# Deep cross network, last layer: one row tile from its own x, another's sums laid into its bank

## The chip, the cores and the metric

The kernel runs on one core of a Trainium2 chip. The metric is device time in microseconds (us) of one launch. Times of the kernel before: 128.68 us median of 3 runs (128.41 to 128.70).

## The reference

Six cross layers on a batch of 4096 rows with 416 features, all in bfloat16:

```python
B, F, D, L = 4096, 26, 16, 6
Din = min(F * D, 1024)          # 416
def reference(x0, ws, bs):      # (4096, 416), (6, 416, 416), (6, 416)
    x = x0
    for l in range(ws.shape[0]):
        x = x0 * (x @ ws[l] + bs[l]) + x
    return x
```

Written out, the state after layer l is x0 times (1 + the sum over the layers so far of x_i W_i + b_i). The kernel before uses this form throughout: it adds the products of all layers up in PSUM and never clears them between layers.

## The kernel before, in words

**Blocks and layout.** The batch is cut into four blocks of 1024 rows (`s` = 0 to 3), each in two halves of 512 rows (`h`). In a block the state is kept transposed: features on partitions, rows along the free dimension. 416 features are three chunks of 128 (`c`) and a tail of 32; the four quarters of a block's tails share 128 partitions. One block after the other passes through all six layers (`l`). Block 3 passes through five of them in this layout; its last layer is written by hand behind the loop.

**A layer.** `main` (L319) multiplies a chunk of W by the state into the bank of half h and chunk m, `bank(h, m)`, banks 0 to 5; `tail_rows` (L335) adds the tail's part to all banks; `tail_outs` (L377) computes the tail's own outputs in banks 6 and 7. `leave` (L428, instruction at L435) on VectorE reads a bank, adds the sum of biases so far (plus one), multiplies by x0 and writes the next state `xT_sb`. `leave_tail` (L450) does the same for the tail: two ScalarE reads (L445) and a GpSimd product (L458).

**The last layer of block 3.** It gives rows on partitions, so that the result can be stored as it is. Block 3's sums of layers 0 to 4, which stand transposed in banks 0 to 5, are first copied with the bias to `sS_sb` by `keep_sum` (L464, instructions at L467 and L469), and the tail's to `st_sb` on GpSimd (L584). For each of eight row tiles of 128 rows (`j`), `row_main` (L617) computes x W into one bank, `row_sums` (L627) adds the tile's old sums to it by multiplying `sS_sb` by an identity matrix, which turns them, and `row_tails` (L639) adds the tail's part to all eight tiles. `finish` (L661) multiplies by x0's rows (`xr_sb`) and writes `o_sb`: on VectorE for six of the tiles (L665), and through a ScalarE copy (L672) and a GpSimd product (L676) for tiles 1 and 3. `store_rows` (L680) sends the rows out on the sync queue or ScalarE's.

**Order.** Every operation is put in a list of its engine by `Plan.add`, in the order in which the program calls it; each engine runs its list in that order. Waits come from the keys that an operation reads and writes. Readers of one PSUM bank also wait for each other. A DMA waits on the engine that issues it. In the last layer the written order on TensorE is: `row_main` of tiles 0 to 3 (in 32-column pieces), `row_sums` of the same, `row_tails`, then `row_main` and `row_sums` of each of the tiles 4 to 7, whole.

**The sync queue.** Blocks 0 to 2 leave through DMA transposes: three of 128x1024 (L475), one of 128x256 for the tails (L480), later a store of 832 KB (L492). The next blocks come in by transposes from DRAM (L205, L211).

Instruction lines in the profile are those of the lines inside the functions; all matmuls of the layers have line L287.

Of the kernel before, what the change touches and what calls it, by code (L numbers as in the profile page):

```python
# [6 lines left out]
FP32 = mybir.dt.float32  # L7
ALU = mybir.AluOpType
ACTF = mybir.ActivationFunctionType
# [109 lines left out]
def bass_standalone__dcn_v2_cross__recsys_kernel(  # L119
# [6 lines left out]
    B, D = x0.shape  # L126
    L = ws.shape[0]
    NC = 3
    DF = 128 * NC
# [3 lines left out]
    NS = B // SB  # L133
    H = SB // 2
# [5 lines left out]
    CH = range(NC)  # L140

    with ExitStack() as es:

        def sb(name, shape, dt=BF16):
            return es.enter_context(nc.sbuf_tensor(name, shape, dt))
# [7 lines left out]
        xr_sb = sb("xr_sb", [128, JS, D])  # L153
        x0T_sb = sb("x0T_sb", [128, NC, B])
        x0t_sb = sb("x0t_sb", [128, NS, 2, G])
        xT_sb = sb("xT_sb", [128, 2, NC, SB])
        xt_sb = sb("xt_sb", [128, 2, 2, G])
        t32_sb = sb("t32_sb", [128, 2, G], FP32)
        sS_sb = sb("sS_sb", [128, NC, SB])
        st_sb = sb("st_sb", [128, G])  # L160
        f32_sb = sb("f32_sb", [128, 2, D], FP32)
        xo_sb = sb("xo_sb", [128, NS - 1, NC, SB])
        xot_sb = sb("xot_sb", [128, NS - 1, G])
        ot_sb = sb("ot_sb", [128, NS - 1, 2, 128])
# [19 lines left out]
        def bank(h, m):  # L184
            return NC * h + m


        def load(queue, dst, src, name, writes):
            P.add(queue, lambda e: e.dma_start(dst, src), writes=writes, dma=name)
# [76 lines left out]
            ), reads=[("ones",)], writes=[("u",)],  # L266
        )
        P.add("gpsimd", lambda e: e.memset(wc_sb[:, :, :], 0.0), writes=[("wc", "wt%d" % i) for i in range(3)])

        def replicate():  # L270
            for g, eng in ((1, "gpsimd"), (3, "scalar"), (2, "gpsimd")):
# [156 lines left out]
        def leave(s, l, h, c):  # L428
            if l == L - 1:
                dst, key = xo_sb[:, s, c, h * H:(h + 1) * H], ("xo", s, c, h)  # L430
            else:
                dst, key = xT_sb[:, (l + 1) % 2, c, h * H:(h + 1) * H], ("xT", (l + 1) % 2, c, h)
            o = s * SB + h * H
            P.add(
                "vector", lambda e: e.scalar_tensor_tensor(  # L435
                    out=dst, in0=ps[:, bank(h, c), :], scalar=cb_sb[:, c, l:l + 1], in1=x0T_sb[:, c, o:o + H],
                    op0=ALU.add, op1=ALU.mult,
                ), reads=[("ps", bank(h, c)), ("cb",), ("x0T", s, c, h)], writes=[key],
            )
# [22 lines left out]
                swap(xt_sb[:, (l + 1) % 2], key, ("scalar", "gpsimd", "scalar", "gpsimd"))  # L462

        def keep_sum(h, c, eng):  # L464
            o, i, b = sS_sb[:, c, h * H:(h + 1) * H], ps[:, bank(h, c), :], cb_sb[:, c, L - 1:L]
            if eng == "scalar":
                fn = lambda e: e.activation(out=o, in_=i, func=ACTF.Identity, bias=b)  # L467
            else:
                fn = lambda e: e.tensor_scalar_add(o, i, b)  # L469
            P.add(eng, fn, reads=[("ps", bank(h, c)), ("cb",)], writes=[("sS", c, h)])  # L470

        def transpose_block(s):
            for c in CH:
# [10 lines left out]
        def store_block(s):  # L484
            P.add(
                "gpsimd", lambda e: e.tensor_copy(
                    out=o_sb[:, s * JS:(s + 1) * JS, DF:D].rearrange("p (g r) f -> p r g f", r=2),
                    in_=ot_sb[:, s, :, :].rearrange("p r (g f) -> p r g f", f=DR),
                ), reads=[("ot", s)], writes=[("oc", s)],
            )  # L490
            P.add(
                "sync", lambda e: e.dma_start(out_v[:, s * JS:(s + 1) * JS, :], o_sb[:, s * JS:(s + 1) * JS, :]),  # L492
                reads=[("o", s), ("oc", s)], writes=[("out", s)], dma="out%d" % s,
            )
# [48 lines left out]
        for s in range(NS):  # L543
            for l in range(L):
                ending = s == NS - 1 and l == L - 2
                if s == NS - 1 and l == L - 1:
                    break
                if s == 0 and l == 0:
                    for k in CH:
                        for part in range(2) if k == 0 else (None,):  # L550
                            for m in CH:
                                main(s, l, 0, m, k, part)
                        if k == 1:
                            tail_in()
                            bias_sums()
                    tail_rows(s, l, True)
                    for c in CH:
                        leave(s, l, 0, c)
                    tail_outs(s, l, False)
                else:  # L560
                    for m in CH:
                        for k in CH:
                            main(s, l, 0, m, k)
                    tail_rows(s, l, l == 0)
                    for c in CH:
                        leave(s, l, 0, c)
                    tail_outs(s, l, False)
                if s == 0 and l == 1:
                    corner(2, L, "wt2")
                leave_tail(s, l, not ending)  # L570
                if l == 2 and 0 < s < NS - 1:
                    place_tail(s + 1)
                if s == 0 and l == 0:
                    corner(1, 2, "wt1")
                if l == 3 and s > 0:
                    store_block(s - 1)
                if ending:
                    P.add(
                        "gpsimd", lambda e: e.tensor_tensor(
                            out=bt_sb[:, :], in0=cb_sb[:, NC, L - 1:L], in1=cb_sb[:, NC, L - 2:L - 1], op=ALU.subtract  # L580
                        ), reads=[("cb",)], writes=[("bt",)],
                    )
                    P.add(
                        "gpsimd", lambda e, t=t32_sb[:, l % 2, :]: e.tensor_scalar_add(st_sb[:, :], t, bt_sb[:, :]),  # L584
                        reads=[("t32", l % 2), ("bt",)], writes=[("st",)],
                    )
                    for c in CH:
                        keep_sum(0, c, "scalar")
                for m in CH:
                    for k in CH:  # L590
                        main(s, l, 1, m, k)
                    leave(s, l, 1, m)
                if ending:
                    for c in CH:
                        keep_sum(1, c, ("scalar", "scalar", "vector")[c])
            if s < NS - 1:
                transpose_block(s)
            if s < NS - 2:
                load_transposed(s + 2, 0, SB)
                load_last_columns(s + 2)  # L600
            if s == NS - 2:
                load("sync", xr_sb[:, :, :], x0_v[:, (NS - 1) * JS:NJ, :], "xr", [("xr",)])


        s, l = NS - 1, L - 1
        ROW_BANKS = (6, 7, 0, 1, 2, 3, 4, 5)
        src, off = src_main(s, l)
        srct, tkey = src_tail(s, l)

# [17 lines left out]
        def row_sums(j, narrow):  # L627
            b, h = ROW_BANKS[j], j // 4

            def fn(pe):  # L630
                for c in CH:
                    ins = row_mm(
                        pe, ps[:, b, c * 128:(c + 1) * 128], sS_sb[:, c, j * 128:(j + 1) * 128], ident[:, :], False, narrow
                    )
                return ins

            P.add("tensor", fn, reads=[("ident",)] + [("sS", c, h) for c in CH], adds=[("ps", b)])
# [23 lines left out]
        def finish(j, by_pool):  # L661
            b, jj = ROW_BANKS[j], (NS - 1) * JS + j
            if by_pool is None:
                P.add(
                    "vector", lambda e: e.tensor_tensor(  # L665
                        out=o_sb[:, jj, :], in0=ps[:, b, 0:D], in1=xr_sb[:, j, :], op=ALU.mult
                    ), reads=[("ps", b), ("xr",)], writes=[("ol", j)],
                )
                return
            t = f32_sb[:, by_pool, :]  # L670
            P.add(
                "scalar", lambda e: e.activation(out=t, in_=ps[:, b, 0:D], func=ACTF.Copy),  # L672
                reads=[("ps", b)], writes=[("f32", by_pool)],
            )
            P.add(
                "gpsimd", lambda e: e.tensor_tensor(out=o_sb[:, jj, :], in0=t, in1=xr_sb[:, j, :], op=ALU.mult),  # L676
                reads=[("f32", by_pool), ("xr",)], writes=[("ol", j)],
            )

        def store_rows(queue, a, b):  # L680
            ja = (NS - 1) * JS
# [2 lines left out]
                reads=[("ol", j) for j in range(a, b)], writes=[("outl", a)], dma="outl%d" % a,  # L684
            )

        for j in range(4):
            row_main(j, True, True)
        for j in range(4):
            row_sums(j, True)  # L690
        row_tails()
        finish(0, None)
        finish(1, 0)
        finish(2, None)
        finish(3, 1)
        for j in range(4, 8):
            row_main(j, False, False)
            row_sums(j, False)
            finish(j, None)
        STORES = (("scalar", 2, 3), ("sync", 0, 2), ("sync", 4, 6), ("sync", 3, 4), ("scalar", 6, 7), ("sync", 7, 8))  # L700
        for queue, a, b in STORES:
            store_rows(queue, a, b)
        P.add("sync", None, reads=[("out", s) for s in range(NS - 1)] + [("outl", a) for _, a, _ in STORES])
# [30 lines left out]
```

## Time and profile before

| | |
|---|---|
| median of 3 runs | 128.68 us |
| the profiled execution | 128.06 us |
| its span, first to last instruction | 126.6 us |
| TensorE busy | 123.0 us, 97% of the span |
| VectorE busy | 99.6 us, 79% |
| ScalarE busy | 43.6 us, 34% |
| GpSimd busy | 38.8 us, 31% |
| TensorE clock granted | 1.00 |
| chain that ended last, TensorE's share | 97% |

PE is TensorE's matmuls, PEld its weight loads, DVE VectorE, ACT ScalarE, POOL GpSimd, SPq and ACTq the DMA queues of the sync engine and of ScalarE. Times in views are us from the span's start; a mean duration is in ns. A line of a timeline gives the start, the time from the first start to the last end of the instructions merged into it, and their number. The profiled execution's time is its span and 1.46 us around it.

### The profile page before, as it was taken

The page shows a single profiled execution, that of the slowest core. Times are in us where ns is not written, and L with a number is a line of the kernel's source. Part 1 is how long each engine was busy: PE and PEld are TensorE (multiplying, and loading weights), DVE is VectorE, ACT ScalarE, POOL GpSimd, SP SyncE. Part 2 cuts the span into 40 slices and gives each one's busy share as a digit, 9 for nine tenths or more (in the row PEclk, how much of TensorE's full clock was granted, in tenths as well). Part 3 has the DMA queues.
Part 4 walks back from the last instruction along what each step waited for, and adds up shares of the span by engine and source line. Part 5 has one row for each costly group of instructions (what it writes and reads, how often), then busy time and mean ns, then how long its engine had stood idle before and what let it go on. Part 6 is the DMA issues. An engine that isn't in the chain of part 4 may idle for free.

```text
span 126.6 us, 5307 instructions
## 1 busy us (share of the span) xinstructions
PE 123.0 (97%) x2414; PEld 64.3 (51%) x2414; DVE 99.6 (79%) x156; ACT 43.6 (34%) x95; POOL 38.8 (31%) x81
## 2 busy tenths in 40 slices
PE   7999999999999999999999999999999999999991
PEld 5554554554555554545545545545545545555660
DVE  2467978879879779779779789788797797797873
ACT  2342523424205225225205224233223252253820
POOL 6505404314204124144014043152122241350450
PEclk9999999999999999999999999999999999999999
DMA  3998998100059791016037893108009480006117
GB/s 99 237 240 226 292 199 107 28 19 0 8 114 161 167 166 28 22 54 226 0 86 169 68 218 87 31 5 269 5 9 203 80 257 0 5 0 226 49 39 236
DMA packets 34934, 14.03 MB, mean 111 GB/s; under 512 B 25722, under 2 KB 34912, under 8 KB 34912
## 3 DMA queue, kind: packets, MB, share of 16 engines
q1 hardware_dynamic: 33744, 13.20, 47.3%
q10 hardware_dynamic: 1136, 0.49, 1.4%
q8 instruction: 19, 0.31, 1.0%
q14 instruction: 3, 0.02, 0.1%
q0 software_dynamic: 32, 0.01, 0.0%
HBM read 3.79 MB, written 3.41 MB: 57 GB/s over the span
## 4 chain that ended last, share of the span: by engine, by line
PE 97%; DVE 0%; issue 0%
PE ps L287 94%; PE ps L295 2%; PE ps L506 1%; DVE o_sb L665 0%
## 5 line engine op out<-in xcount | busy, mean ns | idle before, releaser
L435 DVE SCALAR_TENSOR_TENSOR xT_sb<-ps,cb_sb,x0T_sb 128x512 bf16<-128x512 f32 x120 | 80.9, 743 | 16.5 <-PE ps L287 16.5
L287 PE MATMUL ps<-xT_sb,w_sb 128*32 128x512 bf16 (+1 forms) x1596 | 84.2, 364 | 0.0
L287 PEld LDWEIGHTS ps<-xT_sb,w_sb 128*32 128x32 bf16 x1596 | 40.9, 97 | 37.2 <-issue 4.0
L445 ACT ACTIVATE t_sb<-ps,cb_sb 64x256 f32<-64x256 f32 x46 | 21.6, 469 | 57.2 <-PE ps L287 56.9
L458 POOL TENSOR_TENSOR xt_sb<-t_sb,x0t_sb 128x256 bf16<-128x256 f32 x20 | 13.4, 671 | 65.2 <-ACT t_sb L445 65.2
L422 ACT ACTIVATE xt_sb<-xt_sb 32x256 bf16<-32x256 bf16 x38 | 15.7, 414 | 15.1 <-POOL xt_sb L458 14.9
L287 PE MATMUL ps<-x0T_sb,w_sb 128*32 128x512 bf16 (+1 forms) x348 | 18.6, 358 | 0.1
L424 POOL COPY xt_sb<-xt_sb 32x256 bf16<-32x256 bf16 x38 | 14.9, 392 | 2.4
L435 DVE SCALAR_TENSOR_TENSOR xo_sb<-ps,cb_sb,x0T_sb 128x512 bf16<-128x512 f32 x18 | 12.1, 743 | 2.5 <-PE ps L287 2.5
L287 PEld LDWEIGHTS ps<-x0T_sb,w_sb 128*32 128x32 bf16 x348 | 8.8, 96 | 7.5 <-issue 0.8
L287 PE MATMUL ps<-xt_sb,wt_sb 32*128 32x512 bf16 (+1 forms) x152 | 11.6, 326 | 0.0
L287 PE MATMUL ps<-xt_sb,wc_sb 32*128 32x256 bf16 x76 | 7.3, 268 | 0.0
L287 PEld LDWEIGHTS ps<-xt_sb,wt_sb 32*128 32x128 bf16 x152 | 2.3, 91 | 8.1 <-DVE xT_sb L435 8.1
L458 POOL TENSOR_TENSOR xot_sb<-t_sb,x0t_sb 128x256 bf16<-128x256 f32 x3 | 2.0, 671 | 9.9 <-ACT t_sb L445 9.9
L287 PE MATMUL ps<-w_sb,xT_sb 128*32 128x416 bf16 (+1 forms) x60 | 5.1, 339 | 0.0
L665 DVE TENSOR_TENSOR o_sb<-ps,xr_sb 128x416 bf16<-128x416 f32 x6 | 3.4, 587 | 1.3 <-PE ps L287 1.0
L287 PEld LDWEIGHTS ps<-xt_sb,wc_sb 32*128 32x128 bf16 x76 | 3.9, 93 | 0.2
L295 PE MATMUL ps<-const-bfloat16-1.0 128*128 128x256 bf16 x14 | 3.1, 414 | 0.8 <-PEq L719 0.8
L516 DVE COPY x0T_sb<-ps 128x256 bf16<-128x256 bf16 x6 | 1.3, 282 | 2.4 <-PE ps L506 2.4
L467 ACT ACTIVATE sS_sb<-ps,cb_sb 128x512 bf16<-128x512 f32 x5 | 3.0, 691 | 0.0
L287 PEld LDWEIGHTS ps<-w_sb,xT_sb 128*32 128x32 bf16 (+1 forms) x60 | 2.3, 97 | 1.4 <-issue 0.2
L676 POOL TENSOR_TENSOR o_sb<-f_sb,xr_sb 128x416 bf16<-128x416 f32 x2 | 1.9, 978 | 2.9 <-ACT f_sb L672 2.9
(43 smaller groups left out, 28.2 us busy)
## 6 DMA issues: line engine op xcount, KB each, us to landing
out_dram<-o_sb SPq DMA_DIRECT2D x3, 832.0 KB, 4.4
w_sb<-in_ws_dram SPq DMA_DIRECT2D x5, 312.0 KB, 3.9
xr_sb<-in_x_dram SPq DMA_DIRECT2D x1, 832.0 KB, 5.1
wt_sb<-in_ws_dram SPq DMA_DIRECT2D x4, 104.0 KB, 3.2
out_dram<-o_sb SPq DMA_DIRECT2D x2, 208.0 KB, 2.2
w_sb<-in_ws_dram SPq DMA_DIRECT2D x3, 104.0 KB, 3.7
xin_sb<-in_x_dram ACTq DMA_DIRECT2D x1, 208.0 KB, 3.4
xin_sb<-in_x_dram SPq DMA_DIRECT2D x1, 208.0 KB, 3.1
```

The source lines that it names most:

```text
L287: return pe.matmul(dst, lhsT=lhsT, rhs=rhs, start=start, stop=True, skip_group_check=True, tile_position=pos,)
L295: ins = pe.matmul(ps[:, 7, 0:256], lhsT=const[:, 0:128], rhs=const, start=True, stop=True)
L422: fn = lambda e, d=dst, s=src: e.activation(out=d, in_=s, func=ACTF.Copy)
L424: fn = lambda e, d=dst, s=src: e.tensor_copy(out=d, in_=s)
L435: "vector", lambda e: e.scalar_tensor_tensor(out=dst, in0=ps[:, bank(h, c), :], scalar=cb_sb[:, c, l:l + 1], in1=x0T_sb[:, c, o:o + H], op ...
L445: "scalar", lambda e, p=p, h=h: e.activation(out=dst[p, :], in_=ps[p, T_BANK[h], 0:G], func=ACTF.Identity, bias=cb_sb[p, NC, l:l + 1]), re ...
L458: "gpsimd", lambda e: e.tensor_tensor(out=dst, in0=t, in1=x0t_sb[:, s, 0, :], op=ALU.mult),
L467: fn = lambda e: e.activation(out=o, in_=i, func=ACTF.Identity, bias=b)
L506: ins = pe.transpose(out=psT[:, b, j * 128:(j + 1) * 128], in_=xin_sb[:, 2 * i + j, c * 128:(c + 1) * 128], identity=ident[:, :],)
L516: "vector", lambda e, d=dst, s=src: e.tensor_copy(out=d, in_=s),
L665: "vector", lambda e: e.tensor_tensor(out=o_sb[:, jj, :], in0=ps[:, b, 0:D], in1=xr_sb[:, j, :], op=ALU.mult), reads=[("ps", b), ("xr",)], ...
L676: "gpsimd", lambda e: e.tensor_tensor(out=o_sb[:, jj, :], in0=t, in1=xr_sb[:, j, :], op=ALU.mult),
```

## The change

In the last layer of block 3, two of the eight row tiles no longer get their old sums from TensorE.

Tile 0 is computed in the reference's own form, x0 (x W + b) + x. Its x is fetched by three DMA transposes of the state (128 rows of each chunk) into `xl_sb`. GpSimd forms z = x0 b in layer 3 of block 3, from a broadcast load of the last bias row, then y = z + x. Tile 0 is finished by ScalarE and GpSimd: product with x0, then the sum with y. The tail columns of y are zero, since the tail's sums are still added by `row_tails`.

Tile 3 (`LAID`) gets its sums by three DMA transposes out of `sS_sb` into `sr_sb`; ScalarE copies them into tile 3's bank, and `row_main` of tile 3 adds to what lies there. It is put behind `row_sums` of tiles 1 and 2.

To this end the sums of half 0 are kept earlier, chunk 2 first, between VectorE's `leave` operations and ahead of the tail's reads on ScalarE, and without the first 128 rows; banks of the row tiles, the engines that finish tiles 0 and 1, and the stores are reordered; the store of block 2 is issued a layer earlier.

```diff
+        P.add("gpsimd", lambda e: e.memset(y_sb[:, 1, DF:D], 0.0), writes=[("yz",)])
+        P.add("gpsimd", lambda e: e.memset(sr_sb[:, DF:D], 0.0), writes=[("srz",)])
...
         def keep_sum(h, c, eng):
-            o, i, b = sS_sb[:, c, h * H:(h + 1) * H], ps[:, bank(h, c), :], cb_sb[:, c, L - 1:L]
+            lo = 0 if h else 128
+            o, i, b = sS_sb[:, c, h * H + lo:(h + 1) * H], ps[:, bank(h, c), lo:H], cb_sb[:, c, L - 1:L]
...
+        def transpose_sums(col):
+            for c in (2, 0, 1):
+                P.add(
+                    "sync", lambda e, c=c: e.dma_start_transpose(
+                        sr_sb[:, c * 128:(c + 1) * 128], sS_sb[:, c, col:col + 128]
+                    ), reads=[("sS", c, 0)], writes=[("sr",)], dma="sr",
+                )
+
+        def transpose_first():
+            for c in CH:
+                P.add(
+                    "sync", lambda e, c=c: e.dma_start_transpose(
+                        xl_sb[:, c * 128:(c + 1) * 128], xT_sb[:, (L - 1) % 2, c, 0:128]
+                    ), reads=[("xT", (L - 1) % 2, c, 0)], writes=[("xl",)], dma="xl",
+                )
...
                     tail_rows(s, l, l == 0)
-                    for c in CH:
-                        leave(s, l, 0, c)
+                    if ending:
+                        leave(s, l, 0, 0)
+                        keep_sum(0, 2, "scalar")
+                        keep_sum(0, 0, "scalar")
+                        leave(s, l, 0, 1)
+                        leave(s, l, 0, 2)
+                        keep_sum(0, 1, "scalar")
+                        transpose_sums(H - 128)
+                        transpose_first()
+                    else:
+                        for c in CH:
+                            leave(s, l, 0, c)
                     tail_outs(s, l, False)
...
-                if l == 3 and s > 0:
+                if s > 0 and l == (3 if s < NS - 1 else 2):
                     store_block(s - 1)
+                if s == NS - 1 and l == 3:
+                    P.add(
+                        "gpsimd", lambda e: e.tensor_tensor(
+                            out=y_sb[:, 0, 0:DF], in0=xr_sb[:, 0, 0:DF], in1=bl_sb[:, :], op=ALU.mult
+                        ), reads=[("xr",), ("bl",)], writes=[("z",)],
+                    )
                 if ending:
...
-                    for c in CH:
-                        keep_sum(0, c, "scalar")
+                    P.add(
+                        "gpsimd", lambda e: e.tensor_tensor(
+                            out=y_sb[:, 1, 0:DF], in0=y_sb[:, 0, 0:DF], in1=xl_sb[:, :], op=ALU.add
+                        ), reads=[("z",), ("xl",)], writes=[("y",)],
+                    )
...
+                load("sync", bl_sb[:, :], bs[L - 1:L, 0:DF].to_broadcast([128, DF]), "bl", [("bl",)])
...
-        ROW_BANKS = (6, 7, 0, 1, 2, 3, 4, 5)
+        ROW_BANKS = (0, 1, 6, 2, 7, 3, 4, 5)
+        LAID = 3
...
+            t, o = f32_sb[:, by_pool, :], o_sb[:, jj, :]
+            mid = o if j else p_sb[:, :]
...
+                "gpsimd", lambda e: e.tensor_tensor(out=mid, in0=t, in1=xr_sb[:, j, :], op=ALU.mult),
+                reads=[("f32", by_pool), ("xr",)], writes=[("ol", j) if j else ("p",)],
+            )
+            if not j:
+                P.add(
+                    "gpsimd", lambda e: e.tensor_tensor(out=o, in0=mid, in1=y_sb[:, 1, :], op=ALU.add),
+                    reads=[("p",), ("y",), ("yz",)], writes=[("ol", j)],
+                )
...
-        for j in range(4):
+        for j in range(LAID):
             row_main(j, True, True)
-        for j in range(4):
+        for j in range(1, LAID):
             row_sums(j, True)
+        P.add(
+            "scalar", lambda e: e.activation(out=ps[:, ROW_BANKS[LAID], 0:D], in_=sr_sb[:, :], func=ACTF.Copy),
+            reads=[("sr",), ("srz",)], writes=[("ps", ROW_BANKS[LAID])],
+        )
+        row_main(LAID, False, True)
         row_tails()
-        finish(0, None)
-        finish(1, 0)
+        finish(0, 0)
+        finish(1, None)
         finish(2, None)
         finish(3, 1)
...
-        STORES = (("scalar", 2, 3), ("sync", 0, 2), ("sync", 4, 6), ("sync", 3, 4), ("scalar", 6, 7), ("sync", 7, 8))
+        STORES = (
+            ("scalar", 1, 3), ("sync", 4, 6), ("scalar", 0, 1), ("sync", 6, 7), ("scalar", 3, 4), ("sync", 7, 8),
+        )
```

More of the change, by code (lines that the diff above doesn't have):

```diff
@@ L160, in bass_standalone__dcn_v2_cross__recsys_kernel @@
         st_sb = sb("st_sb", [128, G])
+        sr_sb = sb("sr_sb", [128, D])
         f32_sb = sb("f32_sb", [128, 2, D], FP32)
+        xl_sb = sb("xl_sb", [128, DF])
+        bl_sb = sb("bl_sb", [128, DF])
+        y_sb = sb("y_sb", [128, 2, D], FP32)
+        p_sb = sb("p_sb", [128, D], FP32)
         xo_sb = sb("xo_sb", [128, NS - 1, NC, SB])
@@ L669, in finish @@
                 return
-            t = f32_sb[:, by_pool, :]
+            t, o = f32_sb[:, by_pool, :], o_sb[:, jj, :]
+            mid = o if j else p_sb[:, :]
             P.add(
@@ L675, in finish @@
             P.add(
-                "gpsimd", lambda e: e.tensor_tensor(out=o_sb[:, jj, :], in0=t, in1=xr_sb[:, j, :], op=ALU.mult),
-                reads=[("f32", by_pool), ("xr",)], writes=[("ol", j)],
-            )
+                "gpsimd", lambda e: e.tensor_tensor(out=mid, in0=t, in1=xr_sb[:, j, :], op=ALU.mult),
+                reads=[("f32", by_pool), ("xr",)], writes=[("ol", j) if j else ("p",)],
+            )
+            if not j:
[3 more added lines that the diff above has]
+                )
         def store_rows(queue, a, b):
```

## The prediction

> **What bounds the kernel now.** I read the page's parts 1 and 4 first, then the chain of waits in order of time, then the timeline of the last 12 us engine by engine, and last the DMA transposes by source line. The end of the chain of waits:
>
> ```profile
> 89.97 33.95 PE ps L287 x660
> 123.94 0.59 DVE o_sb L665
> ```
>
> TensorE is never released by anyone here: 34 us of matmuls without a gap, then one VectorE product. The store that follows is not in this view: it is issued at 124.56, lands at 126.40, and the span ends at 126.55. The end of TensorE's timeline:
>
> ```profile
> 117.56 2.28 PE L287 MATMUL ps<-w_sb,xT_sb 128*32 128x416 bf16 x48
> 119.67 0.84 PE L287 MATMUL ps<-ident,sS_sb 128*32 128x128 bf16 x48
> 120.44 0.35 PE L287 MATMUL ps<-wt_sb,xt_sb 32*128 32x416 bf16 x4
> 120.95 0.70 PE L287 MATMUL ps<-w_sb,xT_sb 128*128 128x416 bf16 x3
> ```
>
> By start times: row_main of four tiles 2.11 us (0.527 a tile), row_sums of four tiles 0.776 (0.194 a tile), row_tails 0.505, then four whole tiles of 0.695. The other engines beside it:
>
> ```profile
> 115.19 4.04 DVE L435 SCALAR_TENSOR_TENSOR xT_sb<-ps,cb_sb,x0T_sb 128x512 bf16<-128x512 f32 x6 [0.84 <-PE ps L287]
> 115.84 0.96 ACT L445 ACTIVATE t_sb<-ps,cb_sb 64x256 f32<-64x256 f32 x2 [2.30 <-PE ps L287]
> 116.83 3.00 ACT L467 ACTIVATE sS_sb<-ps,cb_sb 128x512 bf16<-128x512 f32 x5
> 117.81 0.93 POOL L584 TENSOR_SCALAR st_sb<-t_sb,bt_sb 128x256 bf16<-128x256 f32 x1
> 121.08 0.93 ACT L672 ACTIVATE f_sb<-ps 128x416 f32<-128x416 f32 x2 [1.26 <-PE ps L287]
> 121.68 1.91 POOL L676 TENSOR_TENSOR o_sb<-f_sb,xr_sb 128x416 bf16<-128x416 f32 x2 [2.94 <-ACT f_sb L672]
> ```
>
> ScalarE and GpSimd have slack. GpSimd's last product ends at 123.59 and its store lands at 125.83, 0.57 ahead of the last one. Last, the sync queue's timeline around a block's transposes, and L480 by source:
>
> ```profile
> 64.28 4.01 SPq L475 DMA_TRANSPOSE o_sb<-xo_sb  x3
> 68.33 1.24 SPq L480 DMA_TRANSPOSE ot_sb<-xot_sb  x1
> 69.62 4.18 SPq L205 DMA_TRANSPOSE x0T_sb<-in_x_dram  x1
> ```
>
> ```profile
> L480 SPq DMA_TRANSPOSE ot_sb<-xot_sb x3: 1244/1596/1768, 39.0 to 97.6; - x3
> DMA to landing us min/median/max: 2.4/2.8/2.9
> ```
>
> These rows decide the case. L475 transposes 128x1024, L480 only 128x256, and yet L480 holds the queue for 1.24 us, as L475 does (1244 to 1311 ns). The input of that L480 had been ready for microseconds. By the trace's packet times its first packet left 1.256 us after the issue and 0.26 us after the last packet of the transpose before, so it was not held up by a full ring either: the queue was busy making this one.
>
> **What the change takes away.** row_sums of tiles 0 and 3: 2 x 0.194 = 0.39 us of TensorE, on the path. That is the most it can gain, and it is 0.30% of the time; a difference of 0.3% (0.39 us) is about what a measurement of this kernel can tell from none. The other edits cost nothing by themselves: the bias row's load and the product z lie beside work 10 us and more ahead of their use (GpSimd is idle from 114.0 to 116.9); two memsets lie in the head; block 2's store moves one layer (4.9 us) earlier and leaves the sync queue empty; banks are only renamed, and each is read out before its new tile starts (bank 0 by about 116.5 against 117.56, bank 1 by 117.2 against 118.08, bank 6 by 117.6 against 118.61).
>
> **What it adds, in order of time.**
> ScalarE: the sum of chunk 2 can leave when tail_rows has ended (last matmul 115.35), so at 115.41. A 384-column copy lies between L672 (416 columns, 515 ns) and L467 (512 columns, 687 ns), say 0.52: done at 115.93. Chunk 0 waits for VectorE's leave (115.94): done at 116.50. Chunk 1 waits for the next leave (116.60): done at about 117.18. The two tail reads (L445) queue behind that: from 115.84 to about 117.1, 1.25 us later. GpSimd's st slides from 118.74 to about 119.98. TensorE wants it at 120.44 - 0.39 = 120.05 at the earliest, so this is hidden by 0.07 us, and by far more if the next wait is real.
>
> Sync queue: six transposes of 128x128, three of sums and three of x, one after another. The trace has none of this size. Bounds of one issue: 1.24 to 1.31 us if it doesn't depend on size, by L480 and L475; below, by the transposes from DRAM: 12 blocks of 128x128 took 1.93 us, 24 took 3.18, so 0.104 a block, and 7 blocks less than L211's 8 blocks (1.30) would be 0.57. I take 1.244 with 0.04 between issues, 1.285, since L480, with two blocks, is the row nearest in size and kind. Landing: L480 landed 1.17 after its issue ended; with half the packets I take 1.1 (1.0 to 1.4).
> The sums are issued at 115.96, 117.25 and 118.53; the last lands at 118.53 + 1.24 + 1.1 = 120.87.
> The x chunks follow behind them at 119.82, 121.10 and 122.39; the last lands at 122.39 + 1.24 + 1.1 = 124.73.
>
> [...]
>
> First wait: ScalarE lays the transposed sums into bank 2 (0.51 us, as L672): 120.92 to 121.43. TensorE reaches row_main(3) at 119.14 + 0.39 = 119.53 and waits until 121.47, idle 1.94 us. Everything on TensorE is queued behind it. Then row_main 0.53 and row_tails 0.505: the four whole tiles start at 122.50 instead of 120.95, +1.55, and the last VectorE product and its store move with them: end at about 128.1.
>
> Second wait: GpSimd's y = z + x stands ahead of the finishing products in its order, so it holds them until 124.78. Then y (384 columns; L458 takes 671 ns for 256, L676 978 for 416, so 0.92), the product of tile 0 (0.98), the new sum with y (as L676, 0.98; two fp32 inputs may make it slower, I allow 0.3), the product of tile 3 (0.98); with the 0.05 overlap that L676's pair shows between independent ones: 128.6. ScalarE issues tile 3's store there; stores landed 1.85 to 2.2 us after issue (L683), and 0.15 follow to the span's end: 130.6 to 130.95, say 130.75, against 126.55.
>
> Sum: +4.2 us. TensorE's +1.55 lies inside it. The profiled execution took 128.06 in all (span 126.6 and 1.46 around it), 0.62 under the median 128.68. So 128.06 + 4.2 = 132.3 in its own terms, and 132.9 as a median.
>
> **Rivals.**
> *Only the first wait counts (about 130.2).* If y did not have to wait for x, as when the x transposes come out much faster than the sums, the end is TensorE's path, +1.55. Against it: all six are of one size in one queue. Also here lie issues of 0.75 to 1.1 us: the end of GpSimd's chain moves by six times the change in one issue, so 0.9 us gives 132.9 - 2.1 = 130.8. Chance 0.10.
> *The issue shrinks with the size (128.6, no change; the other side).* At 0.57 + 0.04 the sums land at 118.7, before ScalarE is free (the half-1 sums end at 119.3, as L467 shifted); it lays them by 119.77 and TensorE waits 0.28 of the 0.39 saved: -0.11. x lands at 120.5, y ends at 121.5, GpSimd's three operations end at 124.4, and tile 3's store lands at 126.3 to 126.6: the end stays where it is. It decides below an issue of about 0.65 us. For it: the DRAM rows' slope. Against it: L480. Chance 0.11.
> *Faster (128.3).* The whole 0.39 would need the laying to be done by 119.53 and GpSimd's chain, one operation longer, to end no later than before; ScalarE's queue alone puts the laying at 119.77. Chance 0.03.
> *More than 134.* Transposes disturbed as the two slower L480 (1.60, 1.77 us) were, several times over. Chance 0.02.
>
> **How the numbers follow.** The forecast has 0.74: its own bounds are an issue of 1.2 to 1.35 us (six times 0.15), a landing up to 0.3 later, the sum with y up to 0.3 longer, a store 0.2 either way: 132.2 to 133.9. Adding the slower part of the first rival, the range is 130.0 to 133.9. Slower: forecast, first rival and the last, 0.86; no change 0.11; faster 0.03.
>
> **What would show it.** Right: six new transposes on the sync queue of 1.24 to 1.31 us each between 116 and 123.7; TensorE idle some 1.9 us before the fourth tile's row_main, released by ScalarE's copy, which itself waited for a DMA; GpSimd idle until about 124.7 with the reason a DMA into xl_sb; the store of tile 3 the last to land. Wrong: transposes of about 0.6 us, no gap on TensorE at 119.5, and the VectorE product still at the end of the chain; or GpSimd's y started long before 124.

## The result and the profile after

The changed kernel takes 133.16 us (median of 7 runs, 132.84 to 134.73) against 128.57 us before (7 runs): ratio 1.038, 95% interval 1.034 to 1.042, thus 4.6 us slower. The profiled execution shown here is the longest of the seven: 134.73 us in all, span 133.1. It reached the last layer late: row_main of the first tile starts at 118.49 instead of 117.56, and that 0.93 us was lost ahead of the first transpose. In the other profiles shown below the same start lies between 117.48 and 118.43, whatever the version. So times behind it are best compared by their distance from that start.

First the end of the chain of waits, as for the kernel before (start, length, what; its gaps of 0.04 to 0.07 us, called issue, are left out):

```profile
119.78 1.23 SPq L483
121.05 1.23 SPq L491
122.32 1.23 SPq L491
123.60 3.73 DMA xl_sb<-xT_sb
127.41 0.91 POOL y_sb L628
128.32 0.94 POOL p_sb L722
129.32 1.06 POOL o_sb L727
130.38 0.93 POOL o_sb L722
```

TensorE is no longer at its end. The chain goes through the sync queue, transpose after transpose, to the landing of the sixth (the last of x); then GpSimd runs four operations one behind the other, and tile 3's store ends the span. The two groups of transposes by source (duration of the issue in ns, least, median, most; then time to landing):

```profile
L483 SPq DMA_TRANSPOSE sr_sb<-sS_sb x3: 1230/1231/1508, 117.0 to 119.8; - x3
DMA to landing us min/median/max: 2.3/2.4/2.6
```

```profile
L491 SPq DMA_TRANSPOSE xl_sb<-xT_sb x3: 1230/1232/1233, 121.0 to 123.6; - x3
DMA to landing us min/median/max: 2.3/2.4/3.7
```

A transpose of 128x128 holds the queue for 1.23 us (1.51 the first), about as long as the fastest of 128x256 (1.24) and those of 128x1024 (1.24 to 1.31) did before. The timelines of TensorE, ScalarE and GpSimd show the two waits:

```profile
118.49 1.76 PE L294 MATMUL ps<-w_sb,xT_sb 128*32 128x416 bf16 x36
120.08 0.51 PE L294 MATMUL ps<-ident,sS_sb 128*32 128x128 bf16 x24
122.70 1.15 PE L294 MATMUL ps<-w_sb,xT_sb 128*32 128x416 bf16 x12 [2.12 <-ACT ps L743]
```

```profile
122.13 0.52 ACT L743 ACTIVATE ps<-sr_sb 128x416 f32<-128x416 bf16 x1 [1.84 <-DMA sr_sb<-sS_sb]
```

```profile
127.41 0.91 POOL L628 TENSOR_TENSOR y_sb<-y_sb,xl_sb 128x384 f32<-128x384 f32 x1 [6.47 <-DMA xl_sb<-xT_sb]
```

TensorE stands idle for 2.12 us until ScalarE has laid the sums, and ScalarE for 1.84 us until they land. GpSimd is idle for 6.47 us until x lands. In the kernel before, no engine waited for a transfer here. row_main of the laid tile also took 1.15 us instead of 0.7: TensorE's granted clock had fallen to 0.50. In the trace's clock record it falls at 122.83, rises at 126.25 and falls again at 133.07, thus after 3.41 and 6.83 us. Two stretches, each 3.41 us long, on both sides of the first change (columns: busy time and instructions of each engine, then the granted clock, DMA share, GB/s):

```profile
119.42:122.83 3.41, 1.29 (x48) 0.83 (x44) 1.41 (x3) 1.39 (x3) 1.41 (x3) 1.00 0.13 29
122.83:126.25 3.42, 3.42 (x35) 1.40 (x28) 1.10 (x3) 0.93 (x2) 0.00 (x0) 0.50 0.12 24
```

It is granted in full in the stretch of the wait and at one half in the next. This did not set the end here, since tiles 4 to 7 were stored before tile 3 was.

### The profile page after: what moved, and what is told of

Same layout as the page of the kernel before. It is cut to its first block, busy times and chain, and to the rows that moved or that the text cites. A ratio compares the mean times of both kernels' runs of the same rounds, so it can differ in the third digit from the quotient of the medians.

```text
span 133.1 us, 5270 instructions
## 1 busy us (share of the span) xinstructions
PE 125.4 (94%) x2390; PEld 65.4 (49%) x2390; DVE 99.8 (75%) x156; ACT 44.0 (33%) x96; POOL 41.8 (31%) x86
## 3 DMA queue, kind: packets, MB, share of 16 engines
HBM read 3.89 MB, written 3.41 MB: 55 GB/s over the span
## 4 chain that ended last, share of the span: by engine, by line
PE 87%; SPq 3%; POOL 3%; DMA 3%; DVE 1%; ACT 1%; issue 0%
PE ps L294 83%; DMA xl_sb<-xT_sb 3%; PE ps L302 2%; SPq L491 2%; SPq L483 1%; DVE xT_sb L442 1%; PE ps L530 1%; POOL o_sb L727 1%; POOL p_sb L722 1%; POOL o_sb L722 1%; POOL y_sb L628 1%; ACT t_sb L452 1%; ACT sS_sb L475 0%
## 5 line engine op out<-in xcount | busy, mean ns | idle before, releaser
L294 PE MATMUL ps<-x0T_sb,w_sb 128*32 128x512 bf16 (+1 forms) x348 | 19.2, 369 | 0.0
L294 PE MATMUL ps<-w_sb,xT_sb 128*32 128x416 bf16 (+1 forms) x60 | 6.3, 387 | 2.1 <-ACT ps L743 2.1
L475 ACT ACTIVATE sS_sb<-ps,cb_sb 128x384 bf16<-128x384 f32 (+1 forms) x5 | 3.0, 623 | 2.0 <-PE ps L294 1.9
L628 POOL TENSOR_TENSOR y_sb<-y_sb,xl_sb 128x384 f32<-128x384 f32 x1 | 0.9, 909 | 6.5 <-DMA xl_sb<-xT_sb 6.5
```

The costliest lines, as they stand in the source:

```text
L294: return pe.matmul(dst, lhsT=lhsT, rhs=rhs, start=start, stop=True, skip_group_check=True, tile_position=pos,)
L628: "gpsimd", lambda e: e.tensor_tensor(out=y_sb[:, 1, 0:DF], in0=y_sb[:, 0, 0:DF], in1=xl_sb[:, :], op=ALU.add), reads=[("z",), ("xl",)], w ...
```

## The experiments

Theory A: the price is that of issuing, about 1.24 us a transpose whatever its size, six in a row, so that TensorE waits for the third and GpSimd for the sixth. Its rivals: the price goes with the blocks moved, or lies in the landing; only one of the two waits counts. What TensorE's lower clock costs was a question of its own.

**The laid tile alone.** Tile 0 back on TensorE's sums, the x transposes and all that hangs on them gone:

```diff
-                        transpose_first()
...
-            mid = o if j else p_sb[:, :]
+            mid = o
...
-        for j in range(1, LAID):
+        for j in range(LAID):
             row_sums(j, True)
```

> The laid tile 3 alone: tile 0 gets its sums from TensorE again, and the three transposes of x, GpSimd's z and y and the extra sum are gone. Theory A (each transpose holds the queue about 1.24 us whatever its size, TensorE waits for the third one, and its clock falls to half after that wait, as in the changed kernel's profile): the wait stays about 1.9 us, the matmuls behind it run at half clock for some 3 us, and since GpSimd no longer ends last, the whole of that shows: about 132.0 us, ratio 1.026. Theory B (the wait alone counts, the half clock cost nothing that shows): about 130.3 us, ratio 1.013. Theory C (the six transposes of the changed kernel cost only by way of GpSimd's wait for x): about 128.4 us.

Measured 130.22 us, ratio 1.012 (1.007 to 1.017): B's number. The wait is there, at full clock in the profiled execution:

```profile
121.46 0.71 PE L294 MATMUL ps<-w_sb,xT_sb 128*32 128x416 bf16 x12 [1.68 <-ACT ps L725]
```

So the wait for the laid sums costs 1.5 us by itself (130.22 against 128.74), and the other 3 us of the change came through GpSimd; C's 128.4 is far off. That half clock follows the wait in any case, as A's number had it, is refuted: the granted clock was 1.00 in all four executions (0.999 at the least).

**Tile 0 from x alone.** No transposes of sums, no laying:

```diff
-                        transpose_sums(H - 128)
...
-        for j in range(LAID):
+        for j in range(4):
             row_main(j, True, True)
-        for j in range(1, LAID):
+        for j in range(1, 4):
             row_sums(j, True)
...
-        row_main(LAID, False, True)
```

> Tile 0 alone from its own x: tile 3 gets its sums from TensorE again, so the three transposes of x are the only ones, and there is no copy into the bank. Theory A: x lands about 121.0 us from the start instead of 124.7, so y no longer holds GpSimd much; GpSimd's chain, one operation longer, ends near 125.0 and its store lands near 126.9: about 129.0 us, ratio 1.003, TensorE without a gap and at full clock. Rival (the wait for x costs even with three transposes, because landing and not the queue is slow): above 130.5 us.

Measured 128.94 us, ratio 1.001 (0.998 to 1.004), as A said within 0.1 us. GpSimd's timeline:

```profile
121.82 0.91 POOL L627 TENSOR_TENSOR y_sb<-y_sb,xl_sb 128x384 f32<-128x384 f32 x1 [0.94 <-DMA xl_sb<-xT_sb]
122.69 0.98 POOL L721 TENSOR_TENSOR p_sb<-f_sb,xr_sb 128x416 f32<-128x416 f32 x1
```

Three transposes instead of six, and the wait for x shrinks from 6.47 to 0.94 us. The last of these three, issued at 119.41, lands 2.3 us later, like all of the changed kernel's transposes (2.3 to 2.4) but the first (2.6) and the sixth (3.7). So the rival, slow landing, does not hold: most of the difference is the place in the queue, and some 1.4 us the sixth one's late landing, of which more below.

**Two issues in place of six.** The half-0 sums and states of the last layer lie tile by tile, so that three chunks of a tile are contiguous and one transpose takes them:

```diff
+        s0_sb = sb("s0_sb", [128, 4, NC, 128])
+        xn_sb = sb("xn_sb", [128, 4, NC, 128])
...
-            for c in (2, 0, 1):
...
-                        sr_sb[:, c * 128:(c + 1) * 128], sS_sb[:, c, col:col + 128]
...
+                    sr_sb[:, 0:DF].rearrange("p (c f) -> p c f", c=NC), s0_sb[:, 3, :, :].rearrange("p c f -> p (c f)")
...
-            for c in CH:
...
-                        xl_sb[:, c * 128:(c + 1) * 128], xT_sb[:, (L - 1) % 2, c, 0:128]
...
+                    xl_sb[:, :].rearrange("p (c f) -> p c f", c=NC), xn_sb[:, 0, :, :].rearrange("p c f -> p (c f)")
```

> Both parts as in the change, but each group of three 128x128 transposes is one of 128x384; for that the half-0 sums and states of the last layer lie tile by tile. Bytes and blocks moved are the same, issues two in place of six. Theory A (an issue costs 1.24 us whatever its size up to 128x1024): the sums land near 119.7, TensorE waits 0.6 to 0.8 us, x lands near 121.0, GpSimd ends near 125: about 129.1 us, ratio 1.004. Rival (the price goes with the blocks, 1.24 us for each 128x128): nothing moves against the changed kernel, about 133 us.

Measured 128.76 us, ratio 1.001 (0.998 to 1.004): A, and 0.3 us better than it gave. This is the experiment that settles the price. The same bytes in the same blocks, and 4.4 us of the 4.6 are gone. The two issues and TensorE's wait:

```profile
117.92 1.20 SPq L490 DMA_TRANSPOSE sr_sb<-s_sb  x1
119.17 1.25 SPq L497 DMA_TRANSPOSE xl_sb<-xn_sb  x1
```

```profile
120.83 0.71 PE L296 MATMUL ps<-w_sb,xn_sb 128*32 128x416 bf16 x12 [0.50 <-ACT ps L749]
```

What is left of the wait, 0.50 us, takes back more than the 0.39 that the two tiles saved.

**GpSimd's order.** The same transposes and work, but y and tile 0's sum stand behind tile 3's product, and tile 0's store behind tile 3's (the diff shows only the first):

```diff
         finish(3, 1)
+        P.add(
+            "gpsimd", lambda e: e.tensor_tensor(
+                out=y_sb[:, 1, 0:DF], in0=y_sb[:, 0, 0:DF], in1=xl_sb[:, :], op=ALU.add
+            ), reads=[("z",), ("xl",)], writes=[("y",)],
+        )
+        P.add(
+            "gpsimd", lambda e: e.tensor_tensor(
+                out=o_sb[:, (NS - 1) * JS, :], in0=p_sb[:, :], in1=y_sb[:, 1, :], op=ALU.add
+            ), reads=[("p",), ("y",), ("yz",)], writes=[("ol", 0)],
+        )
```

> The change with y and the sum of tile 0 put behind tile 3's product in GpSimd's order, and the two last stores on ScalarE's queue exchanged: the same work and the same transposes, but the two products no longer wait for x. Theory A: the products run at about 124 to 126 us, then y and the sum: the end moves from GpSimd's chain to the later of that (about 130.0) and TensorE's path: 0.6 us less than the changed kernel, about 132.4 us, ratio 1.030. Rival (the wait for x is the whole loss and taking two operations out of it gives 1.9 us back): about 131.2 us, ratio 1.021.

Measured 132.03 us, ratio 1.027 (1.023 to 1.031): 1.1 us less than the changed kernel, between A's 0.6 and the rival's 1.9, nearer to A. The end of its chain of waits:

```profile
123.40 3.57 DMA xl_sb<-xT_sb
126.97 0.07 issue
127.04 0.92 POOL y_sb L743
127.96 0.07 issue
128.03 1.06 POOL o_sb L748
```

The two products that were held up in vain are out of the chain; the landing of x is still in it, and the version stays 3.3 us slower than the kernel before. TensorE's matmuls ended at 126.6 there, at full clock (1.00 from 119.00 to 126.70), after a wait of 2.21 us.

**Matmuls in the wait.** The expectation asks about the clock, and about the loads of instructions, which the trace has among its DMA records: 16 KB each, 0.88 to 1.62 us long in the traces of the kernel before and of the changed one.

```diff
+        fill(16)
         row_main(LAID, False, True)
```

> The change with 16 matmuls on constants (about 107 ns each, 1.7 us) on TensorE in the place of its wait for the laid sums; they write a bank that is cleared later, so the result is the change's. Two things are asked. Clock: if the wait is what lowers it, the granted clock is 1.00 again, and if GpSimd's chain ends last in any case, that by itself changes the time by less than 0.3 us. Load of instructions: the 32 more instructions make TensorE's next load of instructions come earlier than in the changed kernel, where it fell on the sixth transpose and held 8 of its 128 packets for 1.2 us. If that load is a fixed part of the loss there, x lands 1.0 to 1.3 us earlier against the start of the last layer, and the time falls to about 132.0 us (ratio 1.027); if it is chance, the time stays at 133.1 us (1.036).

Measured 133.90 us, ratio 1.040 (1.034 to 1.047). TensorE kept its full clock until its matmuls ended (1.00 from 119.70 to 129.00), and the time didn't fall: the clock was not what the change lost. TensorE's wait shrank to 0.34 us, which didn't help either. The second half of the expectation missed. The delay did move, but onto the sixth issue itself:

```profile
L491 SPq DMA_TRANSPOSE xl_sb<-xT_sb x3: 1232/1232/2365, 120.4 to 122.9; - x3
```

That issue took 2.37 us, and x landed 9.1 us after the start of row_main. Matmuls in the way didn't help, and 32 more instructions didn't get the delay off the transposes.

**The changed kernel twice more.**

> The changed kernel itself, profiled once more, to see which parts of its loss come back. Theory A (six issues of 1.24 us, two loads of instructions that always fall on the first and the last of them, since TensorE's program decides when they come): x lands 8.8 to 9.1 us after the start of row_main again, against 7.2 from the issues alone, and TensorE waits about 2.1 us. Rival (the load on the last transpose was chance): x lands about 7.5 us after the start of row_main. Half clock behind the wait: if it hangs on where the wait falls in a fixed window of time, it comes in some executions and not in others; if on the length of the wait alone, it comes here too.

> The same once more, with the same expectations as for the first repeat: x 8.8 to 9.1 us after the start of row_main by theory A, about 7.5 us by the rival; half clock behind the wait in some of the executions or in all of them.

They took 133.98 and 134.14 us. In both, x landed 8.7 us after the start of row_main (8.8 in the first profile), just under A's range and far from the rival's 7.5; TensorE waited 2.10 and 1.81 us. In the first repeat (r1) the sixth transpose landed 3.6 us after its issue, as in the run with y last (3.6) and in the first profile (3.7), where a load of instructions ran beside it from 124.87 to 126.06; in the second (r2) the sixth issue itself took 2.35 us, as in the run with matmuls in the wait (2.37), and landed 3.9 us after its start in both. So in all five profiles of kernels with six transposes the sixth one landed 3.6 to 3.9 us after its issue, 1.2 us or more above the 2.3 to 2.4 of the others that nothing put off. As a part of the profiled loss this is no chance; that a load of instructions is behind it is shown for the first profile alone. Half clock came in r1 and not in r2. The windows, cut in steps of 3.41 us from the changes of the granted clock, first of r1, then of r2, then of the run with y last:

```profile
119.94:123.35 3.41, 1.31 (x36) 0.58 (x30) 0.31 (x1) 0.68 (x2) 0.42 (x1) 1.00 0.13 29
123.35:126.77 3.42, 3.42 (x15) 1.83 (x15) 2.27 (x4) 0.76 (x2) 0.11 (x1) 0.50 0.27 77
```

```profile
118.51:121.92 3.41, 1.64 (x56) 0.98 (x46) 1.88 (x3) 1.84 (x4) 1.76 (x3) 1.00 0.13 29
121.92:125.33 3.41, 3.37 (x47) 1.97 (x48) 2.08 (x4) 0.93 (x2) 0.00 (x0) 1.00 0.13 27
```

```profile
118.84:122.26 3.42, 1.46 (x52) 0.87 (x41) 1.70 (x3) 1.49 (x3) 1.71 (x3) 1.00 0.12 27
122.26:125.67 3.41, 3.16 (x45) 1.79 (x46) 1.87 (x4) 1.13 (x3) 1.48 (x2) 1.00 0.12 26
```

The first number behind the length is TensorE's busy time. With 1.29 and 1.31 us of a window busy, the next ran at half clock; with 1.46 and 1.64 it did not. The theory that it hangs on where the wait falls held: a wait of 2.21 us (y last) kept the clock, one of 2.10 (r1) lost it.

**Versions without TensorE's wait.** Tile 0 from x by one transpose, tile 3 finished by VectorE, ScalarE's order as before the change:

```diff
-        row_main(LAID, False, True)
...
-        finish(3, 1)
+        finish(3, None)
```

> Tile 0 alone from its own x, fetched by one transpose of 128x384; tile 3 gets its sums from TensorE and is finished by VectorE, so GpSimd finishes only tile 0; ScalarE's order is that of the kernel before. Theory A: x lands near 119.7, nobody waits for it, TensorE saves one tile's sums (0.19 us) and ends last: about 128.5 us, ratio 0.9985, not told from no change. Rival (another engine becomes late: VectorE with seven tiles, or GpSimd): 128.8 us or more, ratio over 1.000.

Measured 128.45 us, ratio 0.998 (0.995 to 1.001). The number is A's, but TensorE is not what ends last. Only GpSimd waited for x, 0.9 us, and nothing at the end hung on it. The chain of waits ends so:

```profile
4.83 115.98 PE ps L296 x2257
120.81 0.02 issue
120.84 3.58 DVE o_sb L711 x7
```

VectorE's seven products run without a gap from 120.84 to the end. It ends 6.94 us after the start of row_main, against 6.97 before: the 0.19 us is taken back by the new bound. This run's single transpose took 1.20 us as well:

```profile
117.20 1.20 SPq L498 DMA_TRANSPOSE xl_sb<-xn_sb  x1
```

That it holds the queue for 1.2 us because it waits for one ahead is ruled out by the run with two issues: its queue issued nothing from 114 to 117.92, and the issue at 117.92 took 1.20 us.

Two tiles from x by one transpose of 128x768:

```diff
+                    xl_sb[:, :, :].rearrange("p j (c f) -> p (j c) f", c=NC),
+                    xn_sb[:, 0:2, :, :].rearrange("p j c f -> p (j c f)")
...
+                out=o_sb[:, (NS - 1) * JS + 1, :], in0=p1_sb[:, :], in1=y_sb[:, 1, 1, :], op=ALU.add
```

> Tiles 0 and 1 from their own x, fetched by one transpose of 128x768; tile 0 is finished by ScalarE and GpSimd, tile 1 by two VectorE operations, tiles 2 and 3 by VectorE with sums from TensorE. Theory A (an issue costs about 1.25 us up to 128x1024): x lands near 119.9, TensorE saves 0.39 us and VectorE, one operation longer, has caught up by the last tile: about 128.35 us, ratio 0.997. Rival (VectorE's extra operation and the late tile 4 come through to the end): 128.7 to 129.0 us, ratio 1.000 to 1.002.

Measured 128.75 us, ratio 1.003 (1.000 to 1.006): the rival's time. The issue of six blocks took 1.23 us again. VectorE, with the extra sum, ends 7.48 us after the start of row_main, against 6.97 before:

```profile
122.18 0.99 DVE L753 TENSOR_TENSOR o_sb<-p_sb,y_sb 128x416 bf16<-128x416 f32 x1
123.10 2.07 DVE L715 TENSOR_TENSOR o_sb<-ps,xr_sb 128x416 bf16<-128x416 f32 x4
```

The same with that product and y in bfloat16:

```diff
-        p1_sb = sb("p1_sb", [128, D], FP32)
+        p1_sb = sb("p1_sb", [128, D])
+        y1_sb = sb("y1_sb", [128, D])
```

> Tiles 0 and 1 from their own x by one transpose, as in the run before it, but the product and y of tile 1 are kept in bfloat16, so that VectorE's sum reads two bfloat16 tiles from SBUF instead of two fp32 ones. That sum took 0.99 us and made VectorE late to the end. Theory A: it takes 0.3 to 0.5 us now, VectorE has caught up by the last tile but for 0.1 us, and TensorE's 0.39 us come through: about 128.2 us, ratio 0.997. Rival (the sum costs the same in bfloat16): ratio 1.003 as before.

Measured 128.54 us, ratio 1.000 (0.999 to 1.002), between the two:

```profile
122.43 0.78 DVE L755 TENSOR_TENSOR o_sb<-p_sb,y_sb 128x416 bf16<-128x416 bf16 x1
123.13 2.07 DVE L717 TENSOR_TENSOR o_sb<-ps,xr_sb 128x416 bf16<-128x416 f32 x4
```

0.78 us instead of the 0.3 to 0.5 expected; VectorE is still the last. But the type is not all that sets these two sums. GpSimd was at work on SBUF tiles beside both, here beside the fp32 one:

```profile
121.76 0.97 POOL L727 TENSOR_TENSOR p_sb<-f_sb,xr_sb 128x416 f32<-128x416 f32 x1
122.81 1.29 POOL L732 TENSOR_TENSOR o_sb<-p_sb,y_sb 128x416 bf16<-128x416 f32 x1
```

VectorE's sum began during GpSimd's product and ended 0.45 us after it (0.23 us in bfloat16). GpSimd's own sum, begun during VectorE's, took 1.29 us, against 1.06 in the changed kernel and 1.08 in bfloat16. So GpSimd's sum was longer beside VectorE's fp32 one. Whether VectorE's was held up as well is not shown: no run here has it without GpSimd beside it, and none shows the 0.3 to 0.5 us expected. No version beat the kernel before by more than can be measured.

## Why the prediction was right, point by point

- **Issue, 1.244 us.** Measured 1230 to 1240 ns in the five profiles with six transposes for all but the first, which took 1.19 to 1.62 us, and the sixth in two of them (2.35 and 2.37). That L480 and not the slope of the transposes from DRAM was the row to go by is shown by the two issues in place of six. No price by the block of 128x128 shows within SBUF: one block cost 1.23 us, three in one transpose 1.20 to 1.26, six 1.23.
- **First wait, 1.94 us, +1.55 at the end.** 2.12, and 2.10 and 1.81 in the repeats; alone, a wait of 1.68 and 1.5 us of time. Right. The prediction named 130.2 for this wait alone, and the laid tile alone gives 130.22.
- **Second wait, x at 124.73.** Mis-sized. That is 7.17 us after the start of row_main; the profiles show 8.7 to 8.8. The term "landing 1.1 us after the issue" held for five of six transposes in the first profile, in r1 and with y last; the sixth was late by 1.2 us and more, in the first profile with a load of instructions beside it, and the first issue was up to 0.4 us longer. In the trace of before, the two slower L480 had such a load beside them (38.55 to 39.56 and 97.14 to 98.29); the prediction gave transposes disturbed like these a chance of 0.02 and kept them out of its sum.
- **GpSimd's chain, 3.8 us from y to the last product's end.** 3.90 in the profile: y 0.91 (forecast 0.92), products 0.97 (0.98), the sum 1.06 (0.98); the 0.3 us allowed for two fp32 inputs was the author's estimate and did not come. The prediction's 1.85 to 2.2 us for the stores' landing was read a little short: the view of L683 has 1.8 to 2.3.
- **The sum.** +4.2 was forecast, +4.6 came (133.16 against 128.57). The mechanism is the one forecast, but that the number fits so well is in part luck, as far as the profiles show. In them the span ends 14.4 to 14.6 us after the start of row_main, against 9.0 before: 5.4 to 5.6 more, not 4.2, and x's late landing (1.5 to 1.7 us) covers the excess. The three profiled executions took 133.98 to 134.73 us, against a forecast of 132.3, and are the longest of the nine of this kernel. The other six took 132.84 to 133.65; whether their sixth transpose was late too is not shown, and that stays open.
- **Hidden work.** st was ready at 120.93, 2.44 us after the start of row_main, as forecast, and nobody waited for it. The half clock was not foreseen; it cost nothing that shows, since tile 3's chain ended later: GpSimd's last product ended 12.7 us after the start of row_main in r1, with half clock, and in r2, without it.
- **The rivals.** Faster was out of reach: 0.39 us is all there is, and even with one transpose for the sums TensorE waited longer than that. The versions without the wait saved it on TensorE, and VectorE, which then ended last, took it back. "More than 134" was meant for several disturbed transposes; in the profiles the sixth alone moved x by 1.2 us and more, and two of the three executions took over 134 us.

## What to carry to other kernels

Price a DMA transpose within SBUF by the issue and not by the bytes: here 1.2 to 1.3 us of its queue for anything from 128x128 to 128x1024 that nothing put off, and 2.3 to 2.5 us to landing up to 128x768. From DRAM the rows of the prediction grow with the size (1.93 us for 12 blocks, 3.18 for 24). Lay the data so that one transpose takes what three would; that alone was worth 4.4 us here. An operation that waits for a late transfer belongs at the end of its engine's order, or the work behind it waits too; that was worth 1.1 us here.

## What the runs showed of the hardware

In these profiles TensorE's granted clock was one half in the windows of 3.41 us behind those with 1.29 and 1.31 us of matmuls, 38% of the window, and full behind those with 1.46 and 1.64. The windows in which TensorE finished agree: behind 2.12 us busy (the first profile) the next was at full clock; behind 0.94 (y last, granted 0.79 from 126.70 to 130.80) at half. For 0.73 (r2) and 1.11 (r1) half clock behind them is an estimate from the mean granted clock of the spans, 0.986 and 0.979.

A load of 16 KB of instructions took 0.88 to 1.62 us in the traces of before and after. In the first profile after, one ran from 124.87 to 126.06; 8 of the sixth transpose's 128 packets left only from 126.05 on, the other 120 by 125.1, and it landed 3.7 us after its issue instead of 2.3 to 2.4.

A VectorE sum of two SBUF tiles (416 columns, fp32) took 0.99 us and with bfloat16 0.78, both with GpSimd at work on SBUF tiles beside it, while a product with one operand from PSUM took 0.58 us beside GpSimd too.
